# Natural feature order for x, whole weight loads and another split of the PSUM banks in a gated-attention and FFN kernel

## The chip, the core and the metric

The kernel runs on one core of one Trainium2 chip. The metric is the device time of one execution in microseconds (us); lower is better. The engines named below are TensorE (PE, with its weight loads listed as PEld), VectorE (DVE), ScalarE (ACT), GpSimd (POOL) and SyncE (SP, which issues the DMAs here).

## The reference

```python
# B, H, S, D = 4, 8, 768, 48
mag = np.sqrt(a_re * a_re + a_im * a_im)
scale = np.minimum(mag, 0.999) / (mag + 1e-06)
for t in range(S):                       # complex state, 48 x 48 per head
    S_re = ar * S_re - ai * S_im + k[t] (outer) v[t]
    S_im = ar * S_im + ai * S_re(old)
    y[t] = q[t] @ S_re
x = y.transpose(0, 2, 1, 3).reshape(B * S, H * D)       # 3072 x 384
out = (((x @ w1) * (x @ w2)) @ w3) @ w_out              # d_ff = 1024
```

All inputs but the four weights are float32; the weights arrive as 8-byte floats and are turned into float32 on the chip.

## The kernel before, in words

**Units.** The work is cut into 8 units: batch b and half h of the sequence, 384 time steps with all 8 heads. A unit has three chunks c of 128 steps. The gates become running products, so that inside a chunk attention is a masked matrix product, and a state T carries over between chunks of one batch.

**Gates (`gates`, L456 to L566).** For each unit a chain of ACT, DVE and POOL steps on 128x1152 tiles makes scaled q and k: logarithm and exponentials, a scan inside chunks (L508), a division step (L517, L518), a scan over angles (L533), sine and cosine, and four products (L549 to L554). Its tiles gA, gR, k, q exist once for even and once for odd units; gZ exists once, so that the chains of two units follow each other. DMAs then lay the results out by head as KL and QL (96 rows: real and imaginary part of 48 features).

**Attention (`scores`, `outputs`).** For a chunk, `scores` turns R and K2 (real and imaginary k) with three PE transposes each into `tp` (L578), which ACT copies to KT (L579); and it makes, in two halves of four heads, scores `sc` (L583), which DVE copies under a mask into A (L584). `outputs` makes y (L601 to L612) from A and V (rows of the chunk) and from QL and T (the past), 32 output features at a time in one of four column positions, copies y to xT (L614), makes `kv` from KT and V (L619) and the next T from it (L623 to L626). The 384 features of x do not stand in natural order: row block 0 and 1 hold features 0 to 31 of heads 0 to 3 and 4 to 7, block 2 the last 16 features of all heads. So w1 and w2 are loaded in the same order, in pieces of 32 or 16 rows (`w12_work`, L689).

**FFN (`ffn_ab`, `ffn_out`).** For a unit, 8 steps j make m = x w1 and m = x w2 (3 matmuls each, L636); ACT copies the first to `a` (L640), DVE multiplies it into ab (L641). Three steps then make `o` with 8 matmuls each (L646) from ab and w3o = w3 w_out, which ACT copies to `ot` (L649) and a DMA writes out.

**Weights.** Before unit 0, w_out and w3 are loaded and converted (`convert`, two ACT and four DVE steps, L670 to L676) and multiplied to w3o (`fuse`, L718); w1 and w2 follow, six pieces of 128x1024. The converted pieces go through three `raw` tiles. Tiles of odd units stand in memory that the conversion gives back when it is done.

**PSUM.** Eight banks: two for sc, one each for tp, y and kv, three for the matmuls m, o and f.

**Order.** Each engine executes its instructions in a fixed order. The order is not the one in which the code is written: a scheduler makes it when the program is built, from the written order, the data and the free tiles. An instruction that waits holds up all behind it on its engine. So the tp, kv, m and o of a unit interleave on PE as the scheduler put them, and the FFN of unit u-1 is issued with the attention of unit u.

Of the kernel before, what the change touches and what calls it, by code (L numbers as in the profile page):

```python
# [20 lines left out]
def general(ctx, tc, qt, kt, v, art, ait, w1s, w2s, w3o, ident, out):  # L21
# [83 lines left out]
    def attention(u):  # L105
# [148 lines left out]
        for g in range(2):  # L254
            hd = 2 * hp + g
            for f0, d0, d1 in ((P * (hd // 4) + 32 * (hd % 4), 0, 32), (2 * P + 16 * hd, 32, D)):
                nc.scalar.copy(out=xn_t[b][:, :, f0:f0 + d1 - d0], in_=ys[:, g, :, d0:d1])
# [58 lines left out]
def kernel(  # L316
# [36 lines left out]

# [32 lines left out]
    ps_1 = fast.enter_context(tc.tile_pool(name="ps_1", bufs=1, space=PSUM))  # L386
    ps_m = fast.enter_context(tc.tile_pool(name="ps_m", bufs=3, space=PSUM))
# [26 lines left out]
    g_t, L_t, xT_t, ab_t, T_t, y_t = {}, {}, {}, {}, {}, {}  # L414
# [13 lines left out]
    def load_qkv(u):  # L428
# [6 lines left out]

        vr = one.tile([P, UC, DM], FP, tag="vr", name="vr")
# [131 lines left out]
    def scores(u, c):  # L568
        QL, KL, R, K2 = L_t[u]
        last = u % 2 and c == UC - 1  # L570
        w = slice(c * C, (c + 1) * C)
        A = Ab[(u * UC + c) % 2]
        KT = None if last else two.tile([P, H, 2, D], FP, tag="KT", name="KT")
        for x, src in enumerate((R, K2)):
            if not last:
                tp = ps_1.tile([P, KD, C], FP, tag="tr", name="tp")
                for f in range(KD):
                    nc.tensor.transpose(out=tp[:, f], in_=src[:, f, w], identity=ident)  # L578
                nc.scalar.copy(out=KT[:, :, x], in_=tp.rearrange("p f c -> p (f c)").rearrange("p (d h) -> p h d", h=H))  # L579
            sc = ps_s.tile([P, H // 2, C], FP, tag="sc", name="sc")  # L580
            for j in range(H // 2):
                hd = x * H // 2 + j
                nc.tensor.matmul(out=sc[:, j], lhsT=KL[:, hd, w], rhs=QL[:, hd, w], start=True, stop=True)  # L583
            nc.vector.copy_predicated(  # L584
                out=A[:, x * H // 2:(x + 1) * H // 2], data=sc,
                mask=causal.rearrange("p (h t) -> p h t", h=1).to_broadcast([P, H // 2, C]))
        y_t[u, c] = A, KT

    def outputs(u, c):
        QL, KL, _, _ = L_t[u]  # L590
        w = slice(c * C, (c + 1) * C)
        A, KT = y_t.pop((u, c))
        V = Vb[u % 2][:, c]
        if c == 0:
            xT_t[u] = two.tile([P, KD, TT], FP, tag="xT", name="xT")
        first = u % 2 == 0 and c == 0
        T = T_t.get(u // 2)
        y = ps_1.tile([P, KD, C], FP, tag="y", name="y")
        for f in range(2):
            for j in range(4):  # L600
                nc.tensor.matmul(out=y[32 * j:32 * j + 32, f], lhsT=V[:, 4 * f + j, 0:LO], rhs=A[:, 4 * f + j],  # L601
                                 start=True, stop=first)
            for j in range(0 if first else 4):
                nc.tensor.matmul(out=y[32 * j:32 * j + 32, f], lhsT=T[:, 4 * f + j, 0:LO], rhs=QL[:, 4 * f + j, w],
                                 start=False, stop=True)
        for i in range(2):
# [8 lines left out]
        if KT is None:  # L615
            return
# [215 lines left out]
```

## Time and profile before

| | us |
|---|---|
| three runs | 704.51, 711.06, 712.73 (median 711.06) |
| the profiled execution | 713.92 |
| its span, first to last instruction | 712.1 |

The profile is of one execution. A row gives an engine's busy time; idle time in front of an instruction is put down to what released it. A matmul of float32 shows as two records in the profile, so 16 `sc` matmuls read as x32. "PEclk" or "granted clock" is the TensorE clock that was granted, as a share of full speed. The names and line numbers are those of the kernel before.

### The profile page before, as it was taken

The page shows a single profiled execution, that of the slowest core. Times are in us where ns is not written, and L with a number is a line of the kernel's source. Part 1 is how long each engine was busy: PE and PEld are TensorE (multiplying, and loading weights), DVE is VectorE, ACT ScalarE, POOL GpSimd, SP SyncE. Part 2 cuts the span into 40 slices and gives each one's busy share as a digit, 9 for nine tenths or more (in the row PEclk, how much of TensorE's full clock was granted, in tenths as well). Part 3 has the DMA queues.
Part 4 walks back from the last instruction along what each step waited for, and adds up shares of the span by engine and source line. Part 5 has one row for each costly group of instructions (what it writes and reads, how often), then busy time and mean ns, then how long its engine had stood idle before and what let it go on. Part 6 is the DMA issues. An engine that isn't in the chain of part 4 may idle for free.

```text
span 712.1 us, 8939 instructions
## 1 busy us (share of the span) xinstructions
PE 589.1 (83%) x3514; PEld 382.9 (54%) x3514; DVE 358.4 (50%) x509; ACT 256.4 (36%) x362; POOL 109.5 (15%) x113
## 2 busy tenths in 40 slices
PE   0087994688907899979989899999899999999996
PEld 0044572244506656745667466755675657667553
DVE  2999828667675582358116830774068503103110
ACT  6664514454745533154044502551345101100110
POOL 4355001012122311121012100320122000000000
PEclk9998997699956999999989999999889999999999
DMA  8896975721979504943009700690092009200001
GB/s 238 274 284 191 177 162 124 154 67 33 108 136 115 110 0 114 123 98 100 0 25 123 188 0 1 93 212 30 0 131 37 12 0 117 41 12 13 13 0 37
DMA packets 45044, 65.77 MB, mean 92 GB/s; under 512 B 4288, under 2 KB 43200, under 8 KB 44224
## 3 DMA queue, kind: packets, MB, share of 16 engines
q1 hardware_dynamic: 44992, 65.10, 46.7%
q8 instruction: 29, 0.48, 0.3%
q14 instruction: 23, 0.19, 0.1%
HBM read 41.42 MB, written 4.72 MB: 65 GB/s over the span
## 4 chain that ended last, share of the span: by engine, by line
PE 55%; DVE 20%; ACT 10%; issue 8%; DMA 4%; SPq 2%; DVEq 0%; ACTq 0%
PE m L636 19%; PE o L646 16%; PE sc L583 7%; PE f L718 4%; PE kv L619 3%; DVE gZ L533 3%; DVE gA L508 2%; PE tp L578 2%; ACT gR L469 2%; ACT gZ L469 2%; DMA q<-in_q_dram 2%; DMA raw<-in_w_dram 2%; DVE cf L675 2%; PE y L601 2%; ACT KT L579 2%
## 5 line engine op out<-in xcount | busy, mean ns | idle before, releaser
L636 PE MATMUL m<-xT,w1s 128*128 128x384 f32 x384 | 143.9, 511 | 17.4 <-DVE w1s L676 10.0
L636 PE MATMUL m<-xT,w2s 128*128 128x384 f32 x384 | 138.2, 496 | 9.8 <-DVE w2s L676 8.6
L646 PE MATMUL o<-w3o,ab 128*128 128x384 f32 x384 | 129.7, 494 | 2.7 <-DVE ab L641 2.7
L636 PEld LDWEIGHTS m<-xT,w1s 128*128 128x128 f32 x384 | 73.3, 197 | 73.4 <-DVE w1s L676 12.6
L636 PEld LDWEIGHTS m<-xT,w2s 128*128 128x128 f32 x384 | 73.9, 194 | 65.5 <-DVE w2s L676 11.0
L584 DVE COPY_PREDICATED A<-causal,sc 128x512 f32<-128x512 int32 x48 | 35.1, 739 | 143.4 <-PE sc L583 143.2
L646 PEld LDWEIGHTS o<-w3o,ab 128*128 128x128 f32 x384 | 72.3, 192 | 50.9 <-DVE ab L641 3.3
L718 PE MATMUL f<-wo_s,w3s 128*128 128x384 f32 x128 | 47.9, 538 | 42.9 <-DVE w3s L676 42.9
L641 DVE TENSOR_TENSOR ab<-m,a 128x384 f32<-128x384 f32 x64 | 35.3, 551 | 94.3 <-PE m L636 91.4
L640 ACT COPY a<-m 128x384 f32<-128x384 f32 x64 | 30.3, 474 | 121.2 <-PE m L636 119.6
L718 PEld LDWEIGHTS f<-wo_s,w3s 128*128 128x128 f32 x128 | 26.7, 212 | 62.2 <-DVE w3s L676 43.5
L583 PE MATMUL sc<-QL,KL 96*128 96x128 f32 x384 | 57.6, 317 | 0.0
L583 PEld LDWEIGHTS sc<-QL,KL 96*128 96x128 f32 x384 | 55.0, 229 | 2.9 <-issue 0.8
L484 POOL TENSOR_TENSOR im<-im,gR 128x1152 f32<-128x1152 f32 (+1 forms) x10 | 20.3, 2041 | 229.6 <-ACT gR L469 194.2
L579 ACT COPY KT<-tp 128x384 f32<-128x384 f32 x40 | 19.2, 479 | 95.9 <-PE tp L578 95.5
L614 ACT COPY xT<-y 128x384 f32<-128x384 f32 x24 | 11.4, 475 | 78.5 <-PE y L612 48.8
L520 POOL TENSOR_TENSOR q<-q,gA 128x1152 f32<-128x1152 f32 (+1 forms) x10 | 28.5, 2847 | 61.4 <-DVE gA L508 48.5
L619 PEld LDWEIGHTS kv<-V,KT 128*96 128x96 f32 x320 | 30.1, 165 | 6.1 <-issue 4.4
L578 PE MATMUL tp<-ident,gR 128*128 128x128 f32 x60 | 12.2, 313 | 25.2 <-DVE gR L549 19.6
L619 PE MATMUL kv<-V,KT 128*96 128x64 f32 x320 | 30.8, 248 | 0.9 <-DVE T L625 0.9
L670 ACT ACTIVATE low<-raw 128x1024 int32<-128x1024 uint32 (+1 forms) x18 | 19.7, 1095 | 22.5 <-DVE cf L675 18.4
L521 POOL TENSOR_TENSOR k<-k,gR 128x1152 f32<-128x1152 f32 (+1 forms) x10 | 23.3, 2341 | 23.5 <-DVE gR L518 23.5
(88 smaller groups left out, 670.3 us busy)
## 6 DMA issues: line engine op xcount, KB each, us to landing
raw<-in_w_dram SPq DMA_DIRECT2D x8, 1024.0 KB, 6.0
KL<-gR SPq DMA_DIRECT2D x24, 193.5 KB, 5.1
KL<-k SPq DMA_DIRECT2D x24, 193.5 KB, 7.9
re<-in_a_re_dram SPq DMA_DIRECT2D x24, 192.0 KB, 9.8
im<-in_a_im_dram SPq DMA_DIRECT2D x24, 192.0 KB, 6.5
k<-in_k_dram SPq DMA_DIRECT2D x24, 192.0 KB, 5.3
q<-in_q_dram SPq DMA_DIRECT2D x24, 192.0 KB, 5.0
vr<-in_v_dram SPq DMA_DIRECT2D x8, 576.0 KB, 5.9
```

The source lines that it names most:

```text
L469: chain(nc.scalar.activation(**kw))
L520: nc.gpsimd.tensor_tensor(out=q[:, s], in0=q[:, s], in1=A[:, s], op=OP.mult)
L578: nc.tensor.transpose(out=tp[:, f], in_=src[:, f, w], identity=ident)
L579: nc.scalar.copy(out=KT[:, :, x], in_=tp.rearrange("p f c -> p (f c)").rearrange("p (d h) -> p h d", h=H))
L583: nc.tensor.matmul(out=sc[:, j], lhsT=KL[:, hd, w], rhs=QL[:, hd, w], start=True, stop=True)
L584: nc.vector.copy_predicated(out=A[:, x * H // 2:(x + 1) * H // 2], data=sc, mask=causal.rearrange("p (h t) -> p h t", h=1).to_broadcast([P ...
L619: nc.tensor.matmul(out=kv[:, hd], lhsT=KT[:, hd], rhs=V[:, hd], start=True, stop=True)
L636: nc.tensor.matmul(out=m, lhsT=w[:, f, j * P:(j + 1) * P], rhs=xT_t[u][:, f], start=(f == 0), stop=(f == KD - 1))
L640: nc.scalar.copy(out=a, in_=got[0])
L641: nc.vector.tensor_tensor(out=ab_t[u][:, j], in0=got[1], in1=a, op=OP.mult)
L646: nc.tensor.matmul(out=m, lhsT=ab_t[u][:, f, t * P:(t + 1) * P], rhs=w3o[:, f], start=(f == 0), stop=(f == KF - 1))
L718: nc.tensor.matmul(out=m, lhsT=w3_t[j][:, f], rhs=wo_s[:, f], start=(f == 0), stop=(f == KF - 1))
```

## The change

x keeps its natural feature order. For that, v of odd heads is written 16 columns later in the 64-column slots of V (columns 16 to 63 instead of 0 to 31 and 48 to 63), so that four neighbouring 32-wide pieces cover 96 features of two heads. `outputs` walks over 12 such pieces ("quads", four of them with two heads) in four lanes, one matmul of each lane in turn, and so mixes the V and T matmuls that stood in blocks. w1 and w2 load as three pieces of 128 rows each. Transposes (`turn`), scores, state and outputs are now functions of their own, placed by a list. PSUM: four banks for m, o and f; two shared by tp, y and kv; two for sc, as before. The number of matmuls of every kind is the same. (`general`, a fallback that these data do not take, changes its copies as well.)

```diff
-    ps_1 = fast.enter_context(tc.tile_pool(name="ps_1", bufs=1, space=PSUM))
-    ps_m = fast.enter_context(tc.tile_pool(name="ps_m", bufs=3, space=PSUM))
+    ps_v = fast.enter_context(tc.tile_pool(name="ps_v", bufs=2, space=PSUM))
+    ps_m = fast.enter_context(tc.tile_pool(name="ps_m", bufs=4, space=PSUM))
...
-        for c in range(UC):
-            nc.gpsimd.tensor_copy(out=V[:, c, :, 0, 0:D], in_=vr[:, c, :, 0])
-            nc.gpsimd.tensor_copy(out=V[:, c, :, 1, 0:LO], in_=vr[:, c, :, 1, 0:LO])
-            nc.gpsimd.tensor_copy(out=V[:, c, :, 1, D:D + HI], in_=vr[:, c, :, 1, LO:D])
+        for i, e0 in enumerate((0, 64 - D)):
+            nc.gpsimd.tensor_copy(out=V[:, :, :, i, e0:e0 + D], in_=vr[:, :, :, i])
...
+    QUADS = [q for h in range(0, H, 2) for q in ([(h, 0)], [(h, 1), (h + 1, 0)], [(h + 1, 1)])]
...
+        lanes = [[] for _ in range(4)]
+        for i, q in enumerate(QUADS):
+            f, j = divmod(i, 4)
+            o = y[32 * j:32 * j + 32, f]
+            got = [(V[:, hd, 32 * e:32 * e + 32], A[:, hd]) for hd, e in q]
+            if not first:
+                got += [(T[:, hd, 32 * e:32 * e + 32], QL[:, hd, w]) for hd, e in q]
+            lanes[j] += [(o, a, b, n == 0, n == len(got) - 1) for n, (a, b) in enumerate(got)]
+        for step in zip(*lanes):
+            for o, a, b, s0, s1 in step:
+                nc.tensor.matmul(out=o, lhsT=a, rhs=b, start=s0, stop=s1)
...
-            hs = words(w).rearrange("(h x e) m -> h e x m", x=1, e=D)
-            for f, (h0, h1, e0, e1) in enumerate(((0, 4, 0, LO), (4, 8, 0, LO), (0, H, LO, D))):
-                srcs = [hs[hd, e0:e1] for hd in range(h0, h1)]
-                got.append(lambda d=d, f=f, srcs=srcs: load_weight(d[:, f:f + 1], srcs))
+        return [lambda d=d, f=f, src=words(w).rearrange("(f p) m -> p f m", p=P): load_weight(d[:, f:f + 1], src[:, f:f + 1])
+                for d, w in ((w1s, w1), (w2s, w2)) for f in range(KD)]
...
+    def pieces(u):
...
+        got = [[tr[0][0]], [tr[0][1]], sc[0], [tr[1][0], kv[0]], [tr[1][1], y[0]], sc[1] + [tr[2][0]], [kv[1], tr[2][1]],
+               [y[1]] + sc[2], [kv[2]], [y[2]]]
+        if u % 2:
+            got[5], got[6], got[8] = sc[1], [kv[1]], []
...
-        for f in interleave(att, ffn(u - 1) if u else []):
-            f()
-            next(steps, None)
+        for i, p in enumerate(pieces(u)):
+            for f in rest[i:i + 1] + p:
+                f()
+                next(steps, None)
```

What the scheduler makes of it is seen at three places.

**DVE between the last conversion of w3 and the first of w1**, with the attention of unit 0 (T and A are its state and masked scores, cf and w1s the conversion). Before:

```order
L676 SCALAR_TENSOR_TENSOR w3s<-mag,cf 128x1024
L623 TENSOR_TENSOR T<-kv,KL 96x512
L625 TENSOR_TENSOR T<-kv,T 96x512
L626 TENSOR_TENSOR T<-T,KL 96x512
L584 COPY_PREDICATED A_85<-causal,sc 128x512 x2
L584 COPY_PREDICATED A_86<-causal,sc 128x512 x2
L584 COPY_PREDICATED A_85<-causal,sc 128x512 x2
L625 TENSOR_TENSOR T<-kv,T 96x512
L626 TENSOR_TENSOR T<-T,KL 96x512
L672 TENSOR_SCALAR cf<-raw 128x1024
```

Now:

```order
L672 SCALAR_TENSOR_TENSOR w3s<-mag,cf 128x1024
L621 TENSOR_TENSOR T<-kv,KL 96x512
L582 COPY_PREDICATED A_85<-causal,sc 128x512 x2
L668 TENSOR_SCALAR cf<-raw 128x1024
L582 COPY_PREDICATED A_86<-causal,sc 128x512
L670 SCALAR_TENSOR_TENSOR cf<-raw,cf 128x1024
L582 COPY_PREDICATED A_86<-causal,sc 128x512
L671 ISA cf<-cf,low 128x2048
L668 TENSOR_SCALAR cf<-raw 128x1024
L672 SCALAR_TENSOR_TENSOR w1s<-mag,cf 128x1024
```

The first step of w1 stood behind six mask copies and four steps of T; now it stands behind two copies and one step of T. The last two mask copies of unit 0 now stand behind the last step of w2. On PE, the transposes and kv that stood between the last f and the first sc of unit 0 stand behind that sc now.

**ACT in the conversion of w2** (low and mag are the conversion's steps, a the FFN's copy, gA the first step of unit 1's gates). Before:

```order
L671 ACTIVATE mag<-raw 128x1024
L640 COPY a<-m 128x384
L670 ACTIVATE low<-raw 128x1024
L671 ACTIVATE mag<-raw 128x1024
L640 COPY a<-m 128x384
L670 ACTIVATE low<-raw 128x1024
L671 ACTIVATE mag<-raw 128x1024
L670 ACTIVATE low<-raw 128x1024
L671 ACTIVATE mag<-raw 128x1024
L469 ACTIVATE gA<-re 128x1152
```

Now:

```order
L666 ACTIVATE low<-raw 128x1024
L667 ACTIVATE mag<-raw 128x1024
L465 ACTIVATE gA<-re 128x1152
L465 ACTIVATE gR<-gA 128x3x384
L465 ACTIVATE gZ,st_low<-re,consts 128x1152 x2
L608 COPY xT<-y 128x3x128
L465 ACTIVATE gZ<-gZ,consts 128x1152
L638 COPY a<-m 128x384
L465 ACTIVATE gZ<-gA,consts 128x1152
L465 ACTIVATE gA<-gA 128x1152
```

No copy of the FFN stands between the conversion's steps any more; the first two stand between steps of unit 1's gates, as others did before.

**PE at the scores of unit 5** (o and ab of unit 4's FFN in front, tp of R and K2). Before, with tile numbers:

```order
L646 MATMUL o_2890<-w3o_60,ab_2509 128x384 x8
L578 MATMUL tp_2921<-ident_61,gR_2522 128x128 x3
L578 MATMUL tp_2932<-ident_61,k_2118 128x128 x3
L578 MATMUL tp_2971<-ident_61,gR_2522 128x128 x3
L578 MATMUL tp_2982<-ident_61,k_2118 128x128 x3
L578 MATMUL tp_3091<-ident_61,gR_2522 128x128 x3
L583 MATMUL sc_2543<-QL_2418,KL_2417 128x128 x4
L583 MATMUL sc_2554<-QL_2418,KL_2417 128x128 x4
L583 MATMUL sc_2593<-QL_2418,KL_2417 128x128 x4
L583 MATMUL sc_2604<-QL_2418,KL_2417 128x128 x4
L601 MATMUL y_2649<-A1_86,V1_88 32x128 x4
```

Now:

```order
L644 MATMUL o_2757<-w3o_60,ab_2441 128x384 x8
L644 MATMUL o_2769<-w3o_60,ab_2441 128x384 x8
L644 MATMUL o_2815<-w3o_60,ab_2441 128x384 x8
L581 MATMUL sc_2510<-QL_2235,KL_2234 128x128 x4
L581 MATMUL sc_2527<-QL_2235,KL_2234 128x128 x4
L607 MATMUL y_2602<-A1_86,V1_88 32x128 x4
L607 MATMUL y_2602<-QL_2235,T_2380 32x128
L607 MATMUL y_2602<-A1_86,V1_88 32x128
L607 MATMUL y_2602<-QL_2235,T_2380 32x128 x2
L607 MATMUL y_2602<-A1_86,V1_88 32x128
L607 MATMUL y_2602<-QL_2235,T_2380 32x128
L581 MATMUL sc_2665<-QL_2235,KL_2234 128x128
```

The transposes no longer stand in a row before the scores: they are spread, three at a time, among the m matmuls and between y matmuls. The y of a chunk now follows its own scores directly, where before the scores of the next chunk stood between. The same holds for units 1, 3 and 7, and with other counts for even units. On ACT, the copy of a unit's third o (L649, now L647) now stands, in units 0 and 2 to 5, behind all `a` copies of the next unit's FFN, so that its bank stays taken during those m; before, it stood ahead of them. At unit 1, DVE has the same order before and after: the mask copies of unit 1 stand behind the last product of unit 2's gates (L554, now L550).

## Rows read from the trace of the kernel before

**Rows 1.** Stretches of time, all engines: us, PE, PEld, DVE, ACT, POOL busy, PEclk, DMA.

```profile
195.00:214.00 19.00, 0.00 (x0) 0.00 (x0) 14.05 (x19) 8.69 (x8) 5.23 (x2) 0.56 0.72 132
...
368.00:443.00 75.00, 69.26 (x450) 46.79 (x451) 35.41 (x49) 25.61 (x37) 10.57 (x12) 0.96 0.45 80
...
587.00:647.00 60.00, 59.40 (x387) 39.69 (x386) 11.52 (x18) 7.84 (x17) 0.00 (x0) 1.00 0.37 54
```

**Rows 2.** Timeline, DVE, conversion: start us, us, instruction [idle before <-releaser].

```profile
102.20 0.74 DVE L584 COPY_PREDICATED A<-causal,sc 128x512 f32<-128x512 int32 x1 [0.17 <-PE sc L583]
...
110.45 0.68 DVE L672 TENSOR_SCALAR cf<-raw 128x1024 int32<-128x1024 int32 x1
...
115.68 0.69 DVE L672 TENSOR_SCALAR cf<-raw 128x1024 int32<-128x1024 int32 x1
...
120.23 0.69 DVE L672 TENSOR_SCALAR cf<-raw 128x1024 int32<-128x1024 int32 x1
...
137.64 1.23 DVE L675 CUSTOM_DVE_ANT_0 cf<-cf,low 128x2048 uint16<-128x2048 uint16 x1 [5.07 <-ACT low L670]
...
143.52 1.23 DVE L676 SCALAR_TENSOR_TENSOR w2s<-mag,cf 128x1024 f32<-128x1024 f32 x1
```

**Rows 3.** Timeline, ACT, conversion of w2 and start of the gates of units 1 and 2.

```profile
136.09 0.48 ACT L640 COPY a<-m 128x384 f32<-128x384 f32 x1 [6.95 <-PE m L636]
...
144.78 1.16 ACT L469 ACTIVATE gA<-re 128x1152 f32<-128x1152 f32 x1 [3.39 <-DVE w2s L676]
...
179.81 1.16 ACT L469 ACTIVATE gA<-re 128x1152 f32<-128x1152 f32 x1
```

**Rows 4.** Timeline, DVE, end of the gates of unit 2.

```profile
217.00 1.35 DVE L554 TENSOR_TENSOR q<-q,gZ 128x1152 f32<-128x1152 f32 x1
```

**Rows 5.** Timeline, PE, units 0 and 1 (a float32 matmul is two records).

```profile
94.92 0.49 PE L578 MATMUL tp<-ident,gR 128*128 128x128 f32 x3
...
100.16 4.00 PE L583 MATMUL sc<-QL,KL 96*128 96x128 f32 x32
...
107.08 0.43 PE L601 MATMUL y<-A,V 128*32 128x128 f32 x8
107.33 0.40 PE L604 MATMUL y<-QL,T 96*32 96x128 f32 x8
...
214.09 0.87 PE L578 MATMUL tp<-ident,gR 128*128 128x128 f32 x3 [19.23 <-DVE gR L549]
...
239.71 0.41 PE L612 MATMUL y<-QL,T 96*32 96x128 f32 x4 [2.36 <-issue]
240.70 3.42 PE L636 MATMUL m<-xT,w1s 128*128 128x384 f32 x6
```

**Rows 6.** Timeline, PE, scores of units 2 to 5 and what stands before them.

```profile
293.23 3.94 PE L583 MATMUL sc<-QL,KL 96*128 96x128 f32 x32
...
367.84 7.06 PE L583 MATMUL sc<-QL,KL 96*128 96x128 f32 x32
...
420.65 1.49 PE L619 MATMUL kv<-V,KT 128*96 128x64 f32 x16
421.99 10.54 PE L646 MATMUL o<-w3o,ab 128*128 128x384 f32 x32
...
442.63 5.48 PE L583 MATMUL sc<-QL,KL 96*128 96x128 f32 x32
...
512.48 6.38 PE L583 MATMUL sc<-QL,KL 96*128 96x128 f32 x32
```

**Rows 7.** Waits of PE from 293 to 707 us: total us, times, longest.

```profile
PE tp L578 <- ACT KT L579: 8.0, 14, 0.6
PE m L636 <- DVE ab L641: 5.0, 5, 1.3
PE y L608 <- issue: 3.3, 1, 3.3
PE y L601 <- ACT xT L614: 2.5, 5, 0.7
```

More of the change, by code (lines that the diff above doesn't have):

```diff
@@ L253, in attention @@
             xn_t[b] = one.tile([P, NC, DM], FP, tag="xn", name="xn")
[L254 to L257, printed above, removed]
+        nc.scalar.copy(
+            out=xn_t[b][:, :, e0:e0 + 2 * D].rearrange("p c (g d) -> p g c d", g=2), in_=ys)
         if u + 2 < NU:
@@ L566, in gates, with turn @@
         yield
-    def scores(u, c):
-        QL, KL, R, K2 = L_t[u]
-        last = u % 2 and c == UC - 1
+    def turn(u, c, x):
+        src = L_t[u][2 + x]
+        if x == 0:
+            KT_t[u, c] = two.tile([P, H, 2, D], FP, tag="KT", name="KT")
+        tp = ps_v.tile([P, KD, C], FP, tag="v", name="tp")
+        for f in range(KD):
+            nc.tensor.transpose(out=tp[:, f], in_=src[:, f, c * C:(c + 1) * C], identity=ident)
+        nc.scalar.copy(out=KT_t[u, c][:, :, x], in_=tp.rearrange("p f c -> p (f c)").rearrange("p (d h) -> p h d", h=H))
@@ L571, in scores @@
+    def scores(u, c, x):
+        QL, KL = L_t[u][0:2]
         w = slice(c * C, (c + 1) * C)
         A = Ab[(u * UC + c) % 2]
[L573 to L586, printed above, removed]
@@ L587, in scores @@
-        y_t[u, c] = A, KT
+        n = H // 2
+        sc = ps_s.tile([P, n, C], FP, tag="sc", name="sc")
+        for j in range(n):
+            nc.tensor.matmul(out=sc[:, j], lhsT=KL[:, x * n + j, w], rhs=QL[:, x * n + j, w], start=True, stop=True)
+        nc.vector.copy_predicated(out=A[:, x * n:(x + 1) * n], data=sc,
+                                  mask=causal.rearrange("p (h t) -> p h t", h=1).to_broadcast([P, n, C]))
+    QUADS = [q for h in range(0, H, 2) for q in ([(h, 0)], [(h, 1), (h + 1, 0)], [(h + 1, 1)])]
@@ L589, in outputs @@
     def outputs(u, c):
-        QL, KL, _, _ = L_t[u]
+        QL = L_t[u][0]
         w = slice(c * C, (c + 1) * C)
-        A, KT = y_t.pop((u, c))
-        V = Vb[u % 2][:, c]
+        A, V = Ab[(u * UC + c) % 2], Vb[u % 2][:, c]
         if c == 0:
             xT_t[u] = two.tile([P, KD, TT], FP, tag="xT", name="xT")
[L596 to L605, printed above, removed]
@@ L606, in outputs @@
-        for i in range(2):
-            for j in range(4):
-                nc.tensor.matmul(out=y[32 * j:32 * j + 32, 2], lhsT=V[:, 2 * j + i, LO:64], rhs=A[:, 2 * j + i],
-                                 start=(i == 0), stop=(first and i == 1))
-        for i in range(0 if first else 2):
-            for j in range(4):
-                nc.tensor.matmul(out=y[32 * j:32 * j + 32, 2], lhsT=T[:, 2 * j + i, LO:64], rhs=QL[:, 2 * j + i, w],
-                                 start=False, stop=(i == 1))
@@ L626, in outputs @@
             nc.vector.tensor_tensor(out=Tn, in0=Tn, in1=rho, op=OP.mult)
-        T_t[u // 2] = Tn
+        T_t[u // 2, n + 1] = Tn
     def ffn_ab(u, j):
@@ L676, in convert, with load_weight @@
         nc.vector.scalar_tensor_tensor(out=dst, in0=mag, scalar=MIN_SQ, in1=f, op0=OP.is_ge, op1=OP.mult)
-    def load_weight(dst, srcs):
-        if srcs[0].dtype != FP:
-            return convert(dst, srcs)
-        n = P // len(srcs)
-        for i, src in enumerate(srcs):
-            nc.sync.dma_start(out=dst[i * n:(i + 1) * n], in_=src)
+    def load_weight(dst, src):
+        if src.dtype == FP:
+            nc.sync.dma_start(out=dst, in_=src)
+        else:
+            convert(dst, src)
     def words(src):
@@ L703, in wo_work @@
         src = words(wo).rearrange("(i p) m -> p i m", p=P)
-        return [lambda i=i: load_weight(wo_s[:, i:i + 2], [src[:, i:i + 2]]) for i in range(0, KF, 2)]
+        return [lambda i=i: load_weight(wo_s[:, i:i + 2], src[:, i:i + 2]) for i in range(0, KF, 2)]
     def w3_work(j):
@@ L786 @@
             pass
-        if u + 1 == NU:
-            judge()
-    for f in ffn(NU - 1):
-        f()
+    unit(0)
+    with ExitStack():
+        for u in range(1, NU):
+            unit(u)
+        judge()
+        for f in ffn(NU - 1):
+            f()
     fast.close()
```

41 lines of the change are left out of this document (22 added, 19 removed).

## The prediction, made before the change was run

> **What bounds the kernel now.** I read the stretches first, then the timeline of PE, then what PE waits for. The last two units have no gates to make; there PE is busy 59.4 of 60 us [rows 1], so about 60 us a unit is what its matmuls cost, and nothing on other engines can matter. In the middle it is different: PE is busy 69.3 of 75 us with a unit of the same matmuls [rows 1], and part of the busy time is slow matmuls. And before unit 1's scores PE does nothing at all for 19 us, with the granted clock at 0.56, near the lower of its two levels, 1.2 of 2.4 GHz [rows 1]: it stands at a transpose for which DVE has not finished the gates of unit 2 [rows 5]. So there are two places for a gain: the chain that leads to that moment (conversion of w1 and w2, gates of unit 1, gates of unit 2), and PE's waits and slow stretches in the steady units.
>
> **The chain at the front.** The reader is to see three things. DVE starts w1's conversion at 110.45, and the last step of w2 ends at 144.75; one piece without a wait takes 4.55 us (115.68 to 120.23) [rows 2], six take 27.3, so 7.0 us are waits, 5.1 of them one wait for ACT [rows 2], which was held by a copy of the FFN's m [rows 3]. Unit 1's gates begin as the last step of w2 ends, at 144.78, since their tiles stand in the conversion's memory; unit 2's begin at 179.81 [rows 3] and end at 218.35 [rows 4]. And unit 1's m begin at 240.70 [rows 5].
>
> *Conversion earlier: -16 us.* In the new order w1's first step stands behind two mask copies, no longer six. The scores of unit 0 move up from 100.16 to the end of f, about 95.1, as the transposes and kv in front of them move behind [rows 5]. The second mask copy ended 2.8 us after the first score (102.20 + 0.74) [rows 2, 5], so the conversion starts at about 97.9. Two more copies and two steps of T lie in between, 0.74 each by the copy's row [rows 2]: 97.9 + 27.3 + 3.0 = 128.2, against 144.75. The big wait should not come back, as no copy of the FFN stands between ACT's conversion steps now. I take -16; if all 7 us of waits come back in another form (a late load, say) it is -9.5. The whole loads themselves I cost at nothing: the same bytes, fewer issues, on a queue that waits for `raw` tiles anyway; DVE hides them, and if DVE's cover were gone the 7 us just named are their price.
>
> *Gates wait more for the FFN: +3 us.* Unit 0's last two mask copies now stand behind w2, so its y, and with it the whole FFN of unit 0, run while unit 1's gates run, and ACT has FFN copies between the steps of the gates. Each such copy can hold a step until three m are through, 3.4 us at low clock [rows 5]. Most fall where the chain waits for DVE anyway. I take one half of that for each of the two units; bounds 0 and +8.
>
> *Unit 1's attention behind the gates: -6.4 us.* The mask copies of unit 1 still stand behind the gates of unit 2 on DVE, so the 19 us stall does not go away: what moves is its end, 218.35 - 13 = 205. What PE had left then was 22.4 us to the first m (218.35 to 240.70 [rows 4, 5]), with transposes that wait for one another, 16 scores at 0.25 us and all else. Now the first 8 scores are done in the gap. Left are two mask copies (1.6), 16 scores (3.9 [rows 6]), 96 y (5.3: four in 0.22 us, by the y rows of unit 0 [rows 5]), a kv (1.3) and two groups of transposes (0.8): 12.9, and 3 us because the clock is low after the gap: 16. Bounds -2 (a wait as the 2.36 us "issue" [rows 5], lower clock for longer) and -9.
>
> *Moved from this FFN to later: -2.3.* Between unit 1's m and unit 2's scores one group of kv (8 matmuls, 1.3 [rows 6]) and two o matmuls (0.65 each [rows 6]) less, a group of transposes (0.3) more.
>
> **The steady units, 293 to 707 us: -9.5 us.** Gone: 14 waits of a transpose for ACT's copy of the one before it, 8.0 us [rows 7], since the groups no longer follow each other; the slow scores of units 3, 4 and 5, which took 7.06, 5.48 and 6.38 us instead of 3.94 [rows 6], 7.1 us in all, as the clock falls while PE idles between transposes; y's waits for its only bank, 2.5 us [rows 7]. Of PE's 5.0 us for DVE's ab [rows 7] I take 1.5: a kv and a transpose now stand between m where the queue was full, but the fourth bank I cost at nothing, as one of the four holds the third o through the next unit's m. In all -19.1. Added: the work moved out of the front, two groups of kv, two of transposes, two o (2.7 + 0.7 + 1.3 = 4.7); y now follows its own scores, so that PE waits for the second mask copy (0.74 and two hand-overs, less the 10 y before it), 0.2 us in each of 18 chunks, more where a 1.4 us gate step stands between the two copies: 3.5; xT of the last chunk, less covered: 0.5; more changes between full-width and 32-wide matmuls: 1. In all +9.7. Bounds -22 and +6.
>
> The changes of width rest on a row: the first eight y records after scores take 0.25 us, the next 0.22 [rows 5], so a change costs about 0.03, and there are some 32 more. The Trainium skill, TensorEngine Tiling (Array Packing), Key Properties, says that a change of tiling mode (not of the tile) drains TensorE; were each drain as long as a score, 0.25 us, this term would be 8 us instead of 1 and the time 687.
>
> **Sum.** -16 + 3 - 6.4 - 2.3 - 9.5 = -31.2 us, from the profiled execution's 713.9 to 682.7. The runs' median, 711.1, is 2.8 under that execution; so 680 us. POOL's two copies of v instead of nine cost nothing: POOL is mostly idle, and the tile is needed a unit later.
>
> **Rivals.** Two per cent, about what this measurement tells from no change, are 14 us: 697 and 725.
>
> *The steady units go to PE's floor (0.17).* If the clock stays up, the waits for ab and the "issue" waits (3.3 in one [rows 7]) do not recur and the copies are in time, another 16 us go: 664. For it: units 6 and 7 run so. Against: they have no gates on DVE.
>
> *The clock still falls (0.12).* The transposes' gaps move to y, and scores stay slow: the 15 us of waits and slow scores change place, 695.
>
> *The front gains nothing (0.10).* ACT is held in the gates by copies that wait for PE, and the 13 us are lost: 693; with the one above, 708. Against: the steps wait for scans for most of that time.
>
> *Slower: mixed lanes lose their overlap (0.06).* The y of four lanes overlap: four in 0.22 us, where a score takes 0.25 alone [rows 5, 6]. Before, V (128 rows) and T (96 rows) came in blocks of four; now they mix in one round. If neighbours of unlike height can not overlap, 32 y cost 7.9 us instead of 1.8, in 20 calls +122: 802. It decides from 3.3 us a call, where it eats the 31 us. Against it: at the borders of the blocks V and T meet now, and the starts go on at 0.22 us [rows 5].
>
> **The numbers.** The forecast has 0.55. Likeliest 680, its own range 668 to 693; with the first three rivals 655 to 704, the slow lanes and the double failure left out. Faster by over 2%: the forecast (with its edge over 697 taken off, 0.52), the first rival, three fifths of the next two, 0.13: 0.82. Slower 0.06, the rest within 2%: 0.12.
>
> **What would show it.** Right: w2's last conversion at 126 to 132 us; unit 2's gates ending near 205; m of unit 1 starting near 221; hardly a wait of a transpose for KT; first scores of units 3 to 5 at 4 us; waits for ab still there. Wrong: conversion steps waiting for a load or for ACT; scores at 6 us; DVE's mask copies behind gate steps, with y waiting over 2 us; 32 y taking over 3 us.

## The result and the profile after

| | us |
|---|---|
| before, four runs | 704.51 to 712.73, median 711.48 |
| changed, four runs | 665.62, 666.08, 666.50, 668.18, median 666.29 |
| ratio | 0.939, 95% interval 0.932 to 0.945 |
| profiled executions, before and changed | 713.92 and 665.62 (span 663.5) |

The change gains 45 us; 31 were forecast, to 680. The forecast's range of 655 to 704 holds the time. Some executions of a kernel are slower than its others (some of the kernel before, one of the features-only kernel with 708.8 us, and two of the one named three and three below, with 696.4 and 2091.8), and all medians and ratios are of the others. The rows below are of one execution of each kernel, and these two are 48.3 us apart. They can be read against one list of landmarks. The last column is what each stretch gave, by the differences of the landmarks.

| landmark, us | before | changed | the stretch up to here |
|---|---|---|---|
| last step of w2's conversion ends | 144.75 | 123.36 | -21.4 |
| gates of unit 2 end | 218.35 | 199.36 | +2.4 |
| unit 1's first m | 240.70 | 215.14 | -6.6 |
| unit 2's first sc | 293.23 | 264.93 | -2.7 |
| PE's last o ends | 706.6 | 657.9 | -20.5 |

**DVE in the conversion**, timeline of the changed kernel, answering to [rows 2]: start, duration, instruction, and in brackets the idle time ahead of it.

```profile
94.68 0.75 DVE L582 COPY_PREDICATED A<-causal,sc 128x512 f32<-128x512 int32 x1 [0.15 <-PE sc L581]
95.31 0.68 DVE L668 TENSOR_SCALAR cf<-raw 128x1024 int32<-128x1024 int32 x1
...
99.77 1.21 DVE L671 CUSTOM_DVE_ANT_0 cf<-cf,low 128x2048 uint16<-128x2048 uint16 x1
100.90 0.68 DVE L668 TENSOR_SCALAR cf<-raw 128x1024 int32<-128x1024 int32 x1
101.50 1.22 DVE L672 SCALAR_TENSOR_TENSOR w1s<-mag,cf 128x1024 f32<-128x1024 f32 x1
...
122.14 1.22 DVE L672 SCALAR_TENSOR_TENSOR w2s<-mag,cf 128x1024 f32<-128x1024 f32 x1
123.27 1.35 DVE L582 COPY_PREDICATED A<-causal,sc 128x512 f32<-128x512 int32 x2
```

Two things are to be seen. The first step of w1 stands behind two mask copies, as planned; before, it stood behind six of them and five steps of T (the text on the change counts four). And at 100.90 the next piece begins before the last step of the piece in front (101.50): two pieces are under way at a time, and no row up to 123.27 has a bracket for ACT or a load. Before, 5.07 us stood in one such bracket [rows 2].

**The chain behind it**, on ACT, DVE and PE (answering to [rows 3 to 6]).

```profile
123.39 1.16 ACT L465 ACTIVATE gA<-re 128x1152 f32<-128x1152 f32 x1 [3.45 <-DVE w2s L672]
...
158.64 1.16 ACT L465 ACTIVATE gA<-re 128x1152 f32<-128x1152 f32 x1
```

```profile
198.01 1.35 DVE L550 TENSOR_TENSOR q<-q,gZ 128x1152 f32<-128x1152 f32 x1
```

```profile
186.39 1.95 PE L581 MATMUL sc<-QL,KL 96*128 96x128 f32 x16
200.06 0.66 PE L607 MATMUL y<-A,V 128*32 128x128 f32 x8 [11.72 <-DVE A L582]
...
215.14 2.20 PE L634 MATMUL m<-xT,w1s 128*128 128x384 f32 x6
...
264.93 1.95 PE L581 MATMUL sc<-QL,KL 96*128 96x128 f32 x16
...
333.24 1.95 PE L581 MATMUL sc<-QL,KL 96*128 96x128 f32 x16
...
399.32 1.95 PE L581 MATMUL sc<-QL,KL 96*128 96x128 f32 x16
...
466.55 1.95 PE L581 MATMUL sc<-QL,KL 96*128 96x128 f32 x16
```

The stall of unit 1 is still there, with another name: not 19.23 us for gR at a transpose [rows 5], but 11.72 for the mask copies, which stand behind the last product of unit 2's gates on DVE. The scores of units 3 to 5 start at full speed (16 records in 1.95 us; 32 took 7.06, 5.48 and 6.38 us before [rows 6]).

**The steady stretch**, from unit 2's scores to PE's end: stretches as in [rows 1], and what PE waited for in it (answering to [rows 7]). Of the kernel before:

```profile
293.20:706.70 413.50, 390.97 (x2477) 258.33 (x2475) 163.76 (x241) 115.07 (x172) 41.22 (x47) 0.97 0.34 58
```

Of the changed kernel:

```profile
264.90:657.90 393.00, 384.27 (x2519) 254.56 (x2517) 169.90 (x243) 117.56 (x179) 37.40 (x20) 1.00 0.37 67
```

```profile
PE m L634 <- DVE ab L639: 5.9, 6, 1.8
PE y L607 <- DVE A L582: 1.1, 2, 0.6
PE m L634 <- ACT xT L608: 0.9, 2, 0.5
PE tp L571 <- ACT KT L572: 0.4, 1, 0.4
```

PE's idle time falls from 22.5 us (413.50 - 390.97) to 8.7, and its busy time by 6.7 although a little more work lies in the stretch; the mean granted clock there rises from 0.97 to 1.00. The 8.0 us for KT are gone, those for ab are not.

### The profile page after: what moved, and what is told of

The parts are those of the page before. It is cut to its first block, busy times and chain, and to the rows that moved or that the text cites. A ratio compares the mean times of both kernels' runs of the same rounds, so it can differ in the third digit from the quotient of the medians.

```text
span 663.5 us, 8788 instructions
## 1 busy us (share of the span) xinstructions
PE 568.1 (86%) x3514; PEld 373.1 (56%) x3514; DVE 360.7 (54%) x509; ACT 255.5 (39%) x362; POOL 94.1 (14%) x57
## 4 chain that ended last, share of the span: by engine, by line
PE 44%; DVE 9%; DMA 6%; ACT 6%; issue 3%; SPq 1%; DVEq 0%; ACTq 0%
PE m L634 20%; PE o L644 14%; PE sc L581 4%; PE y L607 3%; DMA QL<-q 3%; ACT gZ L465 2%; PE kv L617 2%; DVE gA L504 2%; DVE gZ L529 2%; DMA KL<-k 2%; DMA KL<-gR 1%; ACT gR L465 1%; PE tp L571 1%; ACT gA L465 1%; DVE ab L639 1%
## 5 line engine op out<-in xcount | busy, mean ns | idle before, releaser
L634 PE MATMUL m<-xT,w1s 128*128 128x384 f32 x384 | 139.9, 502 | 11.1 <-DVE ab L639 8.7
L634 PE MATMUL m<-xT,w2s 128*128 128x384 f32 x384 | 134.7, 487 | 0.1
L644 PE MATMUL o<-w3o,ab 128*128 128x384 f32 x384 | 126.1, 487 | 0.0
L582 DVE COPY_PREDICATED A<-causal,sc 128x512 f32<-128x512 int32 x48 | 34.9, 732 | 120.1 <-PE sc L581 119.6
L607 PE MATMUL y<-A,V 128*32 128x128 f32 x768 | 47.6, 289 | 31.0 <-DVE A L582 30.9
L607 PEld LDWEIGHTS y<-A,V 128*32 128x32 f32 x768 | 36.3, 114 | 36.9 <-DVE A L582 32.3
L581 PE MATMUL sc<-QL,KL 96*128 96x128 f32 x384 | 51.7, 282 | 0.0
L581 PEld LDWEIGHTS sc<-QL,KL 96*128 96x128 f32 x384 | 46.5, 192 | 7.1 <-issue 4.9
L607 PE MATMUL y<-QL,T 96*32 96x128 f32 x640 | 40.9, 286 | 0.0
L607 PEld LDWEIGHTS y<-QL,T 96*32 96x32 f32 x640 | 34.2, 116 | 0.5 <-issue 0.2
```

Of the source, the lines that this page charges most:

```text
L581: nc.tensor.matmul(out=sc[:, j], lhsT=KL[:, x * n + j, w], rhs=QL[:, x * n + j, w], start=True, stop=True)
L582: nc.vector.copy_predicated(out=A[:, x * n:(x + 1) * n], data=sc, mask=causal.rearrange("p (h t) -> p h t", h=1).to_broadcast([P, n, C]))
L607: nc.tensor.matmul(out=o, lhsT=a, rhs=b, start=s0, stop=s1)
L634: nc.tensor.matmul(out=m, lhsT=w[:, f, j * P:(j + 1) * P], rhs=xT_t[u][:, f], start=(f == 0), stop=(f == KD - 1))
L644: nc.tensor.matmul(out=m, lhsT=ab_t[u][:, f, t * P:(t + 1) * P], rhs=w3o[:, f], start=(f == 0), stop=(f == KF - 1))
```

## The experiments

The first four take the change apart: features with lanes and whole loads; the banks; the written list. PE's columns in the table are of the stretch from unit 2's scores to PE's end. The runs came in sets, with the kernel before beside each; its medians there were 711.5, 712.5, 708.9 and 709.2 us. So the ratio to the kernel beside it is the safer number, and 3 us between kernels of different sets are not resolved.

| kernel | median us | ratio to before (95%) | w2 done | stretch | PE busy | idle | clock |
|---|---|---|---|---|---|---|---|
| before | 711.5 | | 144.8 | 413.5 | 391.0 | 22.5 | 0.97 |
| features only | 697.5 | 0.977 (0.971 to 0.983) | 130.3 | 407.3 | 381.7 | 25.6 | 1.00 |
| banks only | 682.7 | 0.958 (0.954 to 0.963) | 140.4 | 392.7 | 386.4 | 6.3 | 0.99 |
| list only | 724.0 | 1.018 (1.012 to 1.024) | 144.2 | 425.1 | 401.1 | 24.0 | 0.96 |
| features and banks | 669.5 | 0.942 (0.937 to 0.947) | 124.3 | 394.5 | 386.7 | 7.9 | 1.00 |
| changed, all three | 666.3 | 0.939 (0.932 to 0.945) | 123.4 | 393.0 | 384.3 | 8.7 | 1.00 |

**Features only.** The change, with the written order of before instead of the list, and the banks of before:

```diff
-    ps_v = ...(name="ps_v", bufs=2)      # tag "v" for tp, y and kv
-    ps_m = ...(name="ps_m", bufs=4)
+    ps_1 = ...(name="ps_1", bufs=1)      # tags "tr", "y" and "kv"
+    ps_m = ...(name="ps_m", bufs=3)
```

> Of the change only the feature order: v of odd heads 16 columns later, y in lanes, w1 and w2 in whole pieces. PSUM banks and the written order of transposes, scores and states stay as before; PE's order in the steady units stays as before (15 transposes in a row). Theory (the front comes from order on DVE and from the pieces of w1 and w2 being converted two at a time, the steady units from the banks): the conversion still starts behind five mask copies and two steps of T, near 108 to 110 us, but its six pieces lose the 7 us of waits and some gaps, so that w2 ends near 136 and unit 2 starts some 8 us earlier; steady units as before, with transposes waiting about 8 us for KT; about 700 us, 8 to 14 less than before. Rival one (whole loads are what makes the front faster): 21 us earlier, about 688. Rival two (the lanes of y make the steady units faster): the steady stretch falls by over 10 us, about 690. Rival three (lanes cost something that the other parts hide): 32 y take over 2.2 us, 706 or more.

It took 697.5 us, as the theory had it in sum, with w2 done at 130.3 (136 expected) and unit 2's first scores 10.1 us earlier (8 expected). But the steady stretch is 6 us shorter, too, and mostly not at the lanes: the waits for KT are the same 8.0 us, while PE's busy time falls by 9.3. Counted from each start to the next, 6.9 us of that are in the scores and 1.4 in y. What that is stands in the last section.

**Banks only.** The kernel before with the bank lines of the change. For this run and the next, its code is also cut into the functions of the change; here they are written in the order of before:

```diff
-    ps_1 = ...(name="ps_1", bufs=1)      # tags "tr", "y" and "kv"
-    ps_m = ...(name="ps_m", bufs=3)
+    ps_v = ...(name="ps_v", bufs=2)      # tag "v" for tp, y and kv
+    ps_m = ...(name="ps_m", bufs=4)
```

> Of the change only the PSUM split: two banks shared by tp, y and kv, four for m, o and f. Theory (the steady units gain from the split, because two transposes can no longer follow each other in a row of 15 and are spread among other matmuls): waits of tp for KT fall from 8 us to under 2, scores of units 3 to 5 take 4 us, the steady stretch from unit 2's scores to the end falls from 413 to about 395; the front stays: w1's conversion starts behind six mask copies, ends near 143, and unit 1 stalls as before; about 690 us, 18 to 24 less than before. Rival (the written list of pieces is what spreads the transposes): steady stretch near 410, about 706 us. Second rival (tp, y and kv collide for two banks): y and kv wait for copies by ACT for over 5 us, no gain.

It took 682.7 us; the rivals fall. What PE waited for in its steady stretch, in full but for two rows of 0.2:

```profile
PE y L603 <- issue: 3.1, 3, 2.7
PE kv L625 <- DVE T L631: 1.7, 2, 1.2
PE m L642 <- ACT a L646: 0.8, 2, 0.6
```

No wait for KT is left, and none for ab. In the steady units of its order on PE no more than six transposes stand in a row, where 12 to 15 did. The gain exceeds what was expected since the front gains as well: w2 is done 4 us earlier, and unit 1 has no row of transposes behind its stall (unit 2's scores at 282.4 instead of 293.2).

**List only.** The kernel before with the change's list:

```diff
-        for f in interleave(att, ffn(u - 1) if u else []):
...
+        got = [[tr[0][0]], [tr[0][1]], sc[0], [tr[1][0], kv[0]], [tr[1][1], y[0]], ...
```

> Of the change only the written list: transposes, scores, states and outputs as pieces of their own. Features, loads and banks as before. Theory: with one bank for tp the scheduler still puts 12 to 15 transposes in a row before scores, so tp waits for KT stay at 6 to 9 us and scores stay at 5 to 7 us in units 3 to 5; y is now spread between scores; about 707 us, between 0 and 8 less than before. Rival (the list is what makes the steady units faster): steady stretch 395, about 692 us.

The theory was right about the transposes, and wrong about the sum: it is 12 us slower, and up to 8 less than before was expected. The waits of its steady stretch:

```profile
PE m L642 <- DVE ab L647: 13.7, 6, 3.0
PE tp L575 <- ACT KT L576: 8.1, 14, 0.6
PE m L642 <- ACT a L646: 2.1, 4, 0.9
```

The waits for ab have grown from 5.0 [rows 7] to 13.7. The order on ACT says why: with the list the copy of a unit's third o stands behind all eight copies of m of the next unit, as in the changed kernel. One bank stays taken, and of three banks two are left to m. But only 1.5 of the 11.6 us by which the stretch is longer than before are idle time, since other waits went; 10.1 are busy time, at a mean clock of 0.96.

**Features and banks**, the change without its list:

```diff
-        got = [[tr[0][0]], [tr[0][1]], sc[0], [tr[1][0], kv[0]], [tr[1][1], y[0]], ...
+        att = [att[0], att[1], lambda: att_out(u, 0), att[2], lambda: att_out(u, 1), lambda: att_out(u, 2)]
```

> The change without the written list: feature order with whole loads, and the PSUM split; order of writing as before. Theory (list adds little; front and steady units are gained by these two): w1's conversion starts behind four mask copies, near 97 us, two mask copies stand inside w2's conversion, so it ends near 126; steady stretch near 395; 666 to 674 us. Rival (the list carries a third or more of the gain): 680 or more.

At 669.5 us these two carry all but 3 of the 45 us. The list, 12 us slower on its own, seems to gain 3 beside them (0.6 to 7 between the extreme runs of the two), which the sets do not resolve: the intervals of the two ratios overlap.

**Split loads.** The changed kernel with w1 and w2 loaded in 4, 4 and 8 pieces again:

```diff
+                n = 4 if f < 2 else 8
+                srcs = [src[i * P // n:(i + 1) * P // n, f] for i in range(n)]
```

> The changed kernel, but w1 and w2 come in 4, 4 and 8 loads for each piece again, as before the change; features, lanes, banks and list as changed. DVE's order goes back with it: six mask copies and five steps of T stand before the first step of w1, and the pieces are converted one after the other, no longer two at a time. Theory (the loads' number sets the order on DVE, and with it the front): the first step of w1 near 106 us, the last of w2 near 140 as with the banks alone, instead of 123; the steady units as in the changed kernel; 676 to 683 us. Rival (my prediction's own step, whole loads cost and give nothing): the last step of w2 by 128, 666 to 670 us.

It took 683.7 us (ratio to before 0.966, 0.958 to 0.974), with w2 done at 144.1, both a little later than expected: 17 us are given back by the number of loads alone (19 by the ratios). On DVE the pieces go one after the other again, and the wait of before is back; DVE and ACT in its conversion:

```profile
109.72 0.68 DVE L670 TENSOR_SCALAR cf<-raw 128x1024 int32<-128x1024 int32 x1
...
137.00 1.23 DVE L673 CUSTOM_DVE_ANT_0 cf<-cf,low 128x2048 uint16<-128x2048 uint16 x1 [5.27 <-ACT low L668]
...
142.88 1.23 DVE L674 SCALAR_TENSOR_TENSOR w2s<-mag,cf 128x1024 f32<-128x1024 f32 x1
```

```profile
135.45 0.48 ACT L638 COPY a<-m 128x384 f32<-128x384 f32 x1 [7.14 <-PE m L634]
135.82 1.14 ACT L668 ACTIVATE low<-raw 128x1024 int32<-128x1024 uint32 x1
```

No row of the conversion waits for a load. The loads' number acts through the order that the scheduler makes: with split loads all six mask copies and five steps of T of unit 0 stand ahead of the conversion of w1, and two copies of the FFN's m between ACT's steps for w2.

**Whole loads, nothing else**, in the kernel before:

```diff
-            for f, (h0, h1, e0, e1) in enumerate(((0, 4, 0, LO), (4, 8, 0, LO), (0, H, LO, D))):
+        return [lambda ...: load_weight(d[:, f:f + 1], [src[:, f:f + 1]]) for d, w in ... for f in range(KD)]
```

> The kernel before, with one edit: w1 and w2 load as whole pieces of 128 rows. Leaves out the order of w1's and w2's rows that x needs, so that the product is of other rows; the work is the same. Theory (of the feature order's 16 us all come from the loads' number): conversion two at a time from near 104 us, last step of w2 near 131, total 695 to 702 us like the run with the features alone. Rival one (half or more of it came from y in lanes or from v's two copies): 703 to 708. Rival two (nothing comes from it): 711.

699.4 us (0.990, 0.980 to 0.999; the kernel before took 708.9 beside it). The gain in time is just clear of the noise; w2, done at 129.4 as with the features alone, is plain. So what the features give at the front comes from the loads; lanes and v's copies add nothing there that shows.

**Masks before products.** In the changed kernel, instructions on DVE get an order, without a new wait on other engines:

```diff
+            last = tt(out=Z[:, s], in0=Z[:, s], in1=re[:, s], op=OP.subtract)
+            if u == 2:
+                behind(last, (1, 0), "T")
...
+            if u == 2:
+                behind(got, (1, 1))
...
+                if u != 1 or not 11 < n < 17:
+                    next(steps, None)
```

`behind` puts the last subtraction of unit 2's angles after unit 1's first two masks and T, and its first product after the next masks. For that, five pieces of unit 1 are written without a gate step between them.

> The changed kernel, with DVE told to do unit 1's first two mask copies (and the step of T that y needs) before the last subtraction of unit 2's angles, and the next two before the first product of unit 2's gates. Theory (in front of unit 1's y PE stands 11.7 us for DVE's order alone, not for data): y of unit 1 starts near 190 instead of 200, its m near 206 instead of 215; unit 2's gates end some 3 us later, which nothing waits for; unit 2's scores start near 256; 656 to 660 us. Rival (what is won there is given back, since the gates of units 2 and 3 and their transfers set the later starts): 664 to 667 us.

DVE and PE at unit 1:

```profile
190.43 1.33 DVE L591 COPY_PREDICATED A<-causal,sc 128x512 f32<-128x512 int32 x2
191.64 1.35 DVE L542 TENSOR_TENSOR gZ<-gZ,re 128x1152 f32<-128x1152 f32 x1
197.74 0.75 DVE L591 COPY_PREDICATED A<-causal,sc 128x512 f32<-128x512 int32 x1 [4.75 <-PE sc L590]
```

```profile
191.19 0.66 PE L616 MATMUL y<-A,V 128*32 128x128 f32 x8 [2.56 <-DVE A L591]
```

y starts at 191.2 as expected, but m only at 212.1: PE does y and sc at a granted clock of 0.50 to 0.67 from 191 to 199 us, and DVE now waits for the next scores. 661.3 us, 5 less than the changed kernel, or 3 by the ratios (0.935 and 0.939, whose intervals overlap); unit 2's first scores come 2.8 us earlier. The forecast of 656 to 660 took the whole 9 us.

**Masks of unit 0 too.** The edits of the run before, and the attention of unit 0 written ahead of w2's three pieces:

```diff
+        if i == len(work) - 4:
+            for _ in start:
+                pass
+            for p in pieces(0):
+                for g in p:
+                    g()
```

> As the run before, and the attention of unit 0 is written before the conversion of w2, so that its last two mask copies no longer stand behind the last conversion. Theory: y of unit 0's last chunk comes before 113 us, so m of unit 0 can start as w2 is ready, near 124 instead of 128.8, and the scores of unit 1 start near 182; with the edit of the run before 651 to 656 us. Rival (ACT's copies of the FFN now stand between conversion steps and hold DVE, as in the kernel before the change): w2's last step near 130, 658 us or more.

It took 666.5 us: the rival was right, and the theory missed a second thing. On DVE the conversion waits for ACT again, and unit 1's scores wait for their data:

```profile
122.76 1.43 DVE L681 SCALAR_TENSOR_TENSOR w2s<-mag,cf 128x1024 f32<-128x1024 f32 x1 [0.78 <-ACT mag L676]
```

```profile
184.84 3.75 PE L590 MATMUL sc<-QL,KL 96*128 96x128 f32 x16 [9.32 <-DMA QL<-q]
```

w2 is done at 128.0 (4.7 us later), so unit 1's gates end 4.2 us later (165.7 against 161.5), and QL, which is laid out after them, lands later. m of unit 0 does start at 117.0 instead of 128.8, but nothing is won by it: the chain over DVE, not PE, sets when unit 1 can begin.

**Third copy.** In the changed kernel a and ot share four buffers, where each had two:

```diff
-        a = two.tile([P, TT], FP, tag="a", name="a")
+        a = four.tile([P, TT], FP, tag="ao", name="a")
...
-        o = two.tile([P, DM], FP, tag="o", name="ot")
+        o = four.tile([P, DM], FP, tag="ao", name="ot")
```

> The changed kernel, with the two buffers of a and the two of ot put together to four that both may use (same memory), so that ACT's copy of a unit's third o stands ahead of the next unit's copies of m again and its bank is free during those m. Theory of the prediction (one of the four banks is held by the third o, so the fourth is worth nothing, and m still wait for ab): with that bank back the waits of m for ab fall from 8.7 us in all to under 3; 660 to 664 us. Rival (m wait for ab because DVE has steps of the gates of 1.4 to 5 us in front, whatever the banks): waits stay at 6 us or more, 665 to 668 us.

660.5 us (657.6 to 661.8), 5.8 less than the changed kernel, or 4 by the ratios (0.933 and 0.939). The copy of the third o stands ahead again, and the steady stretch has no wait for ab:

```profile
263.80:652.20 388.40, 382.16 (x2519) 254.36 (x2517) 169.19 (x243) 117.97 (x178) 37.51 (x20) 1.00 0.36 66
```

```profile
PE tp L572 <- ACT KT L573: 3.7, 4, 1.3
PE y L608 <- DVE A L583: 1.3, 3, 0.6
PE m L635 <- ACT xT L609: 0.9, 2, 0.5
```

So DVE's long steps alone do not make m wait: with one bank more PE goes on while they run. The edit also lets up to four copies `a` stand, and no run parts the two in this order; but the banks-only kernel, with two buffers for `a`, four banks and the third copy ahead, has no wait for ab either.

**Both.** The edits of the third copy and of the masks before products, in short:

```diff
+        a, o = four.tile(..., tag="ao", ...)
+            if u == 2: behind(last, (1, 0), "T"); behind(got, (1, 1))
```

> The edit of the run before and that of the run with unit 1's masks before the products of unit 2's gates, which gave 661.3 us. If the two gains are of different places they add: 655 to 659 us. If the rival of the run before holds: 660 to 662 us.

656.4 us (653.2 to 657.1; ratio to before 0.927, 0.922 to 0.933): the two gains add, and this version beats both kernels, the changed one by 10 us (8 by the ratios).

**Three banks for m.** The changed kernel with one bank left empty:

```diff
-    ps_m = ...(name="ps_m", bufs=4)
+    ps_m = ...(name="ps_m", bufs=3)
```

> The changed kernel with three PSUM banks for m, o and f as before the change, two shared by tp, y and kv as changed, and one bank left empty. Theory (the steady gain is that transposes no longer stand in a row, which the two shared banks do alone; the fourth bank is worth nothing): 664 to 669 us, waits of tp for KT under 1 us. Rival (the fourth bank carries part of it: the third o no longer fits and moves behind the next unit's scores, and m wait for ab): waits for ab 12 us or more, 672 to 680 us.

682.5 us (0.965, 0.958 to 0.971): the rival holds, with a range that ends 2 us too low. Its steady stretch, the waits of PE in it, and one of these waits on DVE and PE:

```profile
267.70:674.60 406.90, 392.64 (x2529) 259.25 (x2527) 171.36 (x243) 119.92 (x179) 37.70 (x20) 0.98 0.36 65
```

```profile
PE m L634 <- DVE ab L639: 13.5, 4, 4.5
PE y L607 <- issue: 0.6, 1, 0.6
PE m L634 <- ACT a L638: 0.2, 1, 0.2
```

```profile
434.51 5.12 DVE L529 TENSOR_TENSOR_SCAN gZ<-im 128x384 f32<-128x384 f32 x3
...
440.45 0.55 DVE L639 TENSOR_TENSOR ab<-m,a 128x384 f32<-128x384 f32 x1
```

```profile
441.05 3.42 PE L634 MATMUL m<-xT,w2s 128*128 128x384 f32 x6 [3.04 <-DVE ab L639]
```

The product for ab stands behind a scan of 5.12 us on DVE. PE gets as far as its banks reach, and stands still for 3.04 us. The stretch is 13.9 us longer than with four banks, and only 5.5 of that are idle time. The other 8.4 are busy time: the m behind the wait shown take 3.42 us for six records, which take 2.10 at full clock, and the granted clock from 441 to 445 us is 0.61. Here a wait for ab costs more than it lasts.

**Three and three.** The empty bank goes to tp, y and kv:

```diff
-    ps_v = ...(name="ps_v", bufs=2)
+    ps_v = ...(name="ps_v", bufs=3)
```

> As the run before, but the empty bank goes to tp, y and kv: three shared by them, three for m, o and f. Theory: no better than with the bank left empty, within 3 us of it, since two shared banks already spread the transposes. Rival (tp, y and kv collide for two banks, and that is what still costs): 4 us or more below it.

679.0 us, 3.4 less than the run before, between the 3 of the theory and the 4 of its rival; the two kernels' times overlap (677.9 to 681.8 and 678.8 to 684.8) and the stretch is as long (407.0). So a third shared bank adds nothing that shows in the steady units. That two shared banks keep the transposes apart can be read beside the list alone, which also has three banks for m: there they wait 8.1 us for KT in a stretch of 425.1 us, here not at all. (The features differ as well.)

Put together, the banks that m can really use, which is three or four less the one that a late third copy holds, go with the waits for ab:

| banks left to m | kernels | m for ab, us | stretch, us |
|---|---|---|---|
| 2 | list only; three for m; three and three | 13.7; 13.5; 12.5 | 425.1; 406.9; 407.0 |
| 3, transposes in a row | before; features only; whole loads | 5.0; 7.6; 6.5 | 413.5; 407.3; 411.6 |
| 3 | changed; split loads; masks before products | 5.9; 5.3; 5.5 | 393.0; 395.3; 395.0 |
| 4 | banks only; features and banks; third copy; both | 0; 1.2; 0; 0 | 392.7; 394.5; 388.4; 387.7 |

The kernels whose transposes stand in a row (list only too) pay 8 us of waits for KT besides, and some of them a lower clock.

## Why the prediction was right, and where it missed

**Conversion earlier, forecast -16, measured -21.4.** The mechanism held: two mask copies ahead, no copy of the FFN between ACT's steps. The end lies even ahead of the 126 to 132 us named as the sign of being right. Of the 4.8 us between the forecast end, 128.2, and 123.4, 2.6 lie ahead of w1's first step (95.31 against 97.9). That is mostly f, which ended at 92.9 instead of 95.1; over all runs it ended between 91.3 and 95.8 without going by the edits, so no step explains it. The rest is the pieces: 28.05 us from 95.31 to 123.36 with two copies and two steps of T in it (some 2.8 us), so 4.2 us a piece, where 4.55 was taken. Two pieces at a time leave no gap between a step and the next that needs it.

**"The whole loads themselves I cost at nothing": this step failed.** Split again they cost 17 us, and whole alone they bring w2's end from 144.8 to 129.4. The cover that was named, DVE, was right in that no conversion waits for a load. But the loads' number moves the mask copies and the copies of m, and with split loads the changed kernel keeps 0.6 us of the term above. The -16 were put down to "the new order"; 15.3 of the 21.4 come with the loads alone, and some 6 more with the banks beside them (130.3 with the features, 124.3 with features and banks). The size was in the sum under another name.

**Gates wait more for the FFN, forecast +3, measured +2.4** (73.6 us from unit 1's first step to the end of unit 2's gates, now 76.0). That the FFN's copies are what it waits for, no run shows apart.

**Unit 1's attention, forecast -6.4, measured -6.6** (22.35 us from the gates' end to m, now 15.8). The mask copies stand behind the gates, as said. **Moved work: -2.3, measured -2.7**, with one wait for ab of 2.9 us in it.

**Steady units, forecast -9.5, measured -20.5.** The path was right and the sizes were not. PE's time there, counted from each start to the next and apart from its waits, goes with the terms of the sum like this:

| term | forecast, us | measured, us |
|---|---|---|
| waits for KT; y's waits for xT | -8.0; -2.5 | -7.6; -2.5 |
| slow scores | -7.1 | -6.7 |
| waits of m for ab | -1.5 | +0.9 |
| moved work: kv, o, transposes | +4.7 | +1.7 (+2.9, +1.0, -2.2) |
| second mask copy | +3.5 | +1.1 |
| xT of the last chunk | +0.5 | -0.5 |
| changes of width, in y | +1 | +1.0 |
| not in the sum: "issue" waits; waits for `a`; m | 0 | -4.5; -1.0; -2.3 |

What failed is the other side of the sum: the +9.7 to be added are 3.3, and 7.8 us went that were left in place, the "issue" waits of 3.3 and 1.2 us most of all. Why those did not recur stays open: other kernels with the same list have such waits of 0.6 to 2.3 us. The argument about the waits for ab held: three banks are left of four, as many as before. Giving the bank back is worth 5.8 us, and a kernel with the list and only three banks stands at 682. So "the fourth bank I cost at nothing" is right as a difference to before; it hides that the list takes a bank and the fourth one returns it. And the scores' term came true without being shown to be the change's: the features alone gain 6.9 us in the scores with every transpose still in its row.

For the changes between full-width and 32-wide matmuls 1 us was taken, by 0.25 us against 0.22 (the next row of y starts at 107.55). By the timeline they rise from 32 to 54 in the stretch, so by 22 and not 32, and y takes 1.0 us more than before. Before ran at a lower clock, though; against the features alone, at a clock of 1.00 like the changed kernel, y takes 2.4 us more (32.5 and 34.9). So a change costs some 0.1 us at most, and the row was the better guide than a price of a score each (8 us). The Trainium skill, TensorEngine Tiling (Array Packing), Key Properties, states the drain without a duration; the 2.4 us are a bound for it here.

**The rivals.** "PE's floor" gave 664, nearer to 666 than the forecast. It is two thirds of what happened: of its other 16 us in the steady units 11.0 came, as the clock stayed at 1.00 and the "issue" waits did not recur, but 5.9 us of waits for ab are there. The front gave 6.6 us more than the rival took over from the forecast; that the sum comes near 664 is in part luck. "The clock still falls" did not come true (1.00), nor "the front gains nothing". "Mixed lanes lose their overlap" is refuted: y in lanes, with the features alone, takes 1.4 us less than before, and in the changed kernel 1.0 more, not 122. That the list takes a bank, with 12 us lost where there is no fourth one, was no rival and should have been: the order showed the late copy.

## What to carry to other kernels

Where a scheduler orders the work, cost an edit by the order that it makes, also an edit that only changes how many loads bring the same bytes. Count the banks that a stream of matmuls can use once late copies have taken theirs; then compare the time that they cover with the longest step in the queue of the engine that empties them. And a mask copy or other short step that frees a large engine belongs ahead of long steps for later work, but only as far as the chain that sets the next start is not pushed back.

## What had not been expected of the hardware

The same idle place on PE can cost the clock or not. Ahead of unit 3's scores, the kernel before and the one with the features alone do the same transposes with the same gaps; first the rows of before, then the other, with PE's busy time second and PEclk third from the end:

```profile
364.00:368.00 4.00, 2.26 (x13) 1.43 (x14) 0.00 (x0) 2.11 (x4) 0.00 (x0) 0.98 0.00 0
368.00:372.00 4.00, 4.00 (x19) 4.00 (x20) 1.12 (x2) 3.97 (x7) 2.33 (x1) 0.50 0.00 0
```

```profile
355.00:359.00 4.00, 2.29 (x14) 1.46 (x15) 0.00 (x0) 2.17 (x4) 0.00 (x0) 1.00 0.00 0
359.00:363.00 4.00, 4.00 (x44) 3.75 (x47) 2.40 (x4) 3.97 (x7) 2.39 (x1) 1.00 0.02 6
```

PE is busy for 2.26 and 2.29 of 4 us; then the granted clock is 0.50, the lower of its two levels (1.2 GHz), in the one and 1.00 (2.4 GHz) in the other. So the prediction's "the clock falls while PE idles between transposes" names where it may fall, not that it does. The Trainium skill, TensorE: Matmul & The Clock Gate, What's actually happening, says that the chip's watch on PE's activity runs freely and does not begin with the kernel; the rows agree with that, since as far as they show the places differ only in when they come. Most of what PE's busy time loses with the features alone (9.3 us, 6.9 of it in the scores) may then be luck, and with it the changed kernel's 6.7 us in the scores; with whole loads alone, the same transposes go with 387.6 us of busy time, between the two. It may also be why runs of before spread over 704.5 to 712.7 us and those of the changed kernel, which has no such place, over 665.6 to 668.2; no run here shows that by itself.
